# Block-sparse attention and a gated projection on one core: earlier weights, six decoding steps a unit, key blocks copied by GpSimd in every batch, projection steps spread

## The chip, the cores and the metric

The kernel runs on one core of one Trainium2 chip. The metric is the device time of one execution in microseconds (us). The runs shown of the kernel before took 418.15 to 419.96 us, with a median of 419.37 us. Its profile comes from one further execution.

The core has five engines that run their own instruction streams and wait for each other by semaphores: TensorE (PE in the profile; PEld is its weight load), VectorE (DVE), ScalarE (ACT), GpSimd (POOL) and SyncE (SP), which here only issues transfers. Each engine works through its stream in order.

## The reference

For 4 batches, 8 heads, 768 positions and 64 numbers a head, attention is computed under a mask of 24 x 24 blocks of 32 positions. Then the attention's output goes through a causal convolution of five taps that makes a gate, and through two projections.

```python
mask = np.abs(blk_i - blk_j) <= 1
mask |= (blk_i == 0) | (blk_j == 0) | (blk_i == 23) | (blk_j == 23)
for qb in range(24):
    for kb in sampled_blocks[qb]:          # three drawn blocks
        mask[qb*32:(qb+1)*32, kb*32:(kb+1)*32] = True
scores = np.where(mask, q @ k.T / 8, -1e9)
x = softmax(scores) @ v                    # heads side by side: [4, 768, 512]
gate_pre = sum(conv_w[k] * x_padded[:, k:k+768, :] for k in range(5))
out = (sigmoid(gate_pre) * (x @ w_val)) @ w_out
```

So an inner query block sees at most eight key blocks: the two end blocks, itself and its two neighbours, and three drawn ones. The first and last query block see all 24. The drawn numbers are data: the kernel reads them into registers and fetches or copies the blocks that they name. The weights arrive as 64-bit floating numbers and are turned into pairs of 32-bit numbers (high part and rest) on the chip.

## The kernel before

**Units.** The work on attention is cut into 52 units, the passes of the main loop (lines 622 to 678). A batch has 13: four pairs of query blocks, then two units for the end query blocks (unit 4 and 5 of a batch, for which all 24 key blocks are scored), then seven more pairs. With unit `n` the loop issues: loads for pairs some units ahead; the scores of unit `n`; key copies for unit `n + 2` (`COPY_AHEAD`); the values of unit `n - 2` (`LAG_V`), that is probabilities times `v`; and the transposes of unit `n - 1` (`LAG_T`), two blocks for a pair and three for a unit of the end blocks. Behind each transposed block come one call of `fill()` and one of `prepare(steps)`.

**Keys.** For each pair a tile `kg` holds the key blocks that its two query blocks need. Lines 282 and 283 copy four neighbours on GpSimd, line 288 the end blocks on ScalarE. The six drawn blocks come in two ways, by the table `COPIED` (line 39): in batches 0 and 1 GpSimd copies three and ScalarE three out of the batch's whole keys `bt.k`, which are on the chip anyway; in batches 2 and 3 the table is empty, so SyncE fetches each from memory with a transfer of 64 KB (line 272).

**Values.** A pair's own value rows `va` come through SyncE's queue, the drawn ones `vb` by two gathers on GpSimd (line 305). The batch's whole values `vn`, read only by the units of the end blocks, come in three pieces of 520 KB. `V_BEFORE` names the pairs whose key loads they follow: -1 (the end blocks' entry, loaded together with pair 3), 4 and 5.

**Weights.** `load_weights` (line 175) brings eight blocks of 512 KB, four of `w_val` and four of `w_out`, into four staging tiles. The staging tiles `xh`, `xl`, `yh`, `yl` are those that the projections use later. `WEIGHTS_AT` (line 34) gives the unit from which each may be issued, at most one a unit; blocks 4 to 7 wait besides until the block before them in the same tile is decoded. `decode_weights` (line 187) takes eight VectorE steps for the convolution's weights and eight for each block, 72 in all, and begins a block two units after its issue at the earliest. If the next block is not there by the loop's count, the step is lost.

**Projections.** The 768 positions of a batch are cut into tiles of 384 (in the last batch 384, 256 and 128). When a tile's attention is done, `gates` makes its gate (16 VectorE steps of one tap each, and a few that hold only ScalarE work: the first tap and the tanh), and `split` its high part `xh` on ScalarE and its rest `xl` on GpSimd. Neither begins before all weights are decoded. Then `project` takes 11 steps for 384 positions: four value blocks `vp` of 12 matmuls, and for each 128 rows two half output blocks `op` of 6 matmuls; between them VectorE multiplies by the gate (`y`), ScalarE makes `yh` and GpSimd the rest `yl`. One call of `fill()` advances this by one step, one call of `prepare(steps)` does `steps` steps of decoding or, after it, of gates, and one of `split`.

**What sets the order.** Every instruction is chained to the one before it on its engine (`InOrder`, line 59), so the order written is the order run. How much decoding and projecting stands beside which unit is set by four numbers:

```python
STEPS_FIRST, STEPS, STEPS_TAIL, FIRST = 2, 3, 2, 12   # prepare: 2 a call before unit 12, then 3
HELD = (44, 45, 46, 47)                               # units whose later fill() calls are left out
```

By the loop's own count, decoding ends in unit 16, the first gate begins there, and the first value block `vp` is issued in unit 20. The two last loop passes, 52 and 53, have no scores. The work that is left then runs in the loop of lines 679 to 683, with nothing else beside it.

Of the kernel before, what the change touches and what calls it, by code (L numbers as in the profile page):

```python
# [14 lines left out]
SP, POOL, ACT = mybir.EngineType.SP, mybir.EngineType.Pool, mybir.EngineType.Activation  # L15
# [7 lines left out]
CH = 4  # L23
# [4 lines left out]
RING = 4  # L28
VRING = 3
K_AHEAD = (8, 9, 10)  # L30
V_BEFORE = (-1, 4, 5)
GLOB_AFTER = 3
LAG_T, LAG_V = 1, 2
WEIGHTS_AT = (1, 3, 5, 7, 9, 10, 11, 13)
DECODE_LAG = 2
SCALE_AHEAD = 2
COPY_AHEAD = 2

COPIED = [{0: POOL, 1: POOL, 2: POOL, 3: ACT, 4: ACT, 5: ACT}] * 2 + [{}] * 2

STEPS_FIRST, STEPS, STEPS_TAIL, FIRST = 2, 3, 2, 12

HELD = (44, 45, 46, 47)


@with_exitstack
def attention_moe(ctx, tc, qb, kb, v, sampled, w_val, conv_w, w_out, ident_in, slot_in, out):
# [83 lines left out]
    def indices(b):  # L131

        row = const.tile([128, NB], F32, tag=f"row{b % 2}", name="row")
        dve.tensor_scalar_add(row, base, float(b * S - B * S))
        dve.tensor_tensor(out=row, in0=row, in1=valid, op=ALU.mult)
        dve.tensor_scalar_add(idx[:, b, :], row, float(B * S))
# [36 lines left out]
    staged = []  # L173
# [11 lines left out]
    decoded = set()  # L185
# [58 lines left out]
    def block_numbers(pr, eng):  # L244

        mine = [n for n in range(2 * NR) if COPIED[pr.bt.b].get(n, SP) == eng]
        if not mine:
            return
        first = NR * PAIRS[pr.p][0] + mine[0]
        _, regs = nc.values_load_multi_w_load_instructions(  # L250
            sm[0:1, first : first + len(mine)], engines=[eng], min_val=0, max_val=NB - 1,
            skip_runtime_bounds_check_because="block numbers are drawn from [0, 24)",
        )
        for n, reg in zip(mine, regs):
            yield 5 + 4 * (n // NR) + n % NR, reg

    def load_keys(pr):
# [3 lines left out]
        if pr.p == 0 and b == 0:  # L261
            for _ in range(3):
                next(loading[b])
        if pr.p in V_BEFORE:
            next(loading[b])
# [105 lines left out]
    def transposes(un):  # L371
        un.PT = []
        for p in un.P:
            pt = ps_pt.tile([128, 4, 128], F32, tag="pt", name="pt")
            for c in range(4):
                transpose(pt[:, c, :], p[:, 128 * c : 128 * c + 128], ident)
            t = three.tile([128, 4, 128], F32, tag="ptr", name="ptr")
            act.copy(t, pt)
            un.PT += [t[:, c, :] for c in range(4)]
            yield  # L380
# [169 lines left out]
    def store():  # L550
        while stores:
            sp.dma_start(*stores.pop(0))
# [3 lines left out]
    def advance(jobs, after=None):  # L556

        m, g = jobs[0]
        try:
            next(g)  # L560
        except StopIteration:
            jobs.pop(0)
            if after is not None:
                after(m)

    def queue_rows(bt, t):
        m = Rows()
        m.bt, (m.t, m.n), m.ready, m.begun = bt, TILES[bt.b][t], [], False
        to_gate.append((m, gates(m)))
        to_split.append((m, split(m)))  # L570
# [9 lines left out]
    def fill():  # L580
        if to_project and step[0] > max(to_project[0][0].ready):
            advance(to_project)

    def prepare(steps):
        for _ in range(steps):
            if next(decoding, None):
                continue

            if "all" in decoded and to_gate and (to_gate[0][0].begun or len(gating) < 2):
                to_gate[0][0].begun = True  # L590
                gating.add(id(to_gate[0][0]))
                advance(to_gate, prepared)

        if "all" in decoded and to_split and unread <= {id(to_split[0][0])}:
            advance(to_split, prepared)
# [5 lines left out]
    def freed(k):  # L601

        return units[min(k, N - 1)].pr.seq if k >= 0 else -1

    def more(which, upto, load):
        if at[which] < len(pairs) and pairs[at[which]].seq <= upto:
            load(pairs[at[which]])
            at[which] += 1
            return True

    def until(which, n, do):
        while at[which] < min(len(pairs), pairs.index(units[min(n, N - 1)].pr) + 1):
            do(pairs[at[which]])
            at[which] += 1
# [7 lines left out]
    for n in range(N + LAG_V):  # L622
        step[0] = n

        def more_keys():
            return more("keys", freed(n - 1) + RING, load_keys)

        def more_values():
            return more("values", freed(n - LAG_V - 1) + VRING, load_values)

        if n == 0:
            more_keys()
            numbers_first = {eng: list(block_numbers(pairs[0], eng)) for eng in (POOL, ACT)}
            until("scaled", 0, scale)
            indices(0)
            until("copied", 0, copy_keys)
            more_keys()
            until("copied", 1, copy_keys)
            more_values()
        else:  # L640
            while more_keys() or more_values():
                more_values()
        until("scaled", n + (SCALE_AHEAD if n else 1), scale)
        store()
        k = len(staged)
        if k < 2 * CH and n >= WEIGHTS_AT[k] and (k < 4 or k - 4 in decoded):
            next(weights)

        if n < N:
            scores(units[n])  # L650
        if n == 0:
            more_keys()
        until("copied", n + COPY_AHEAD, copy_keys)
        if n == 0:
            while more_keys() or more_values():
                more_values()
        if 0 <= n - LAG_V < N:
            values(units[n - LAG_V])
        steps = STEPS_FIRST if n < FIRST else STEPS
        if 0 <= n - LAG_T < N:  # L660
            for half, _ in enumerate(transposes(units[n - LAG_T])):
                if not (half and n in HELD):
                    fill()
                prepare(steps)
        else:
            fill()
            prepare(steps)
        if 0 <= n - LAG_V < N and units[n - LAG_V].last:
            pr = units[n - LAG_V].pr
            finish(pr)  # L670
            pr.bt.done.add(pr.p)
            for t, (r0, rn) in enumerate(TILES[pr.bt.b]):
                need = {p for p in range(NP - 1) if any(r0 <= i * BLK < r0 + rn for i in PAIRS[p])}
                if r0 == 0 or r0 + rn == S:
                    need.add(-1)
                if t not in pr.bt.queued and need <= pr.bt.done:
                    pr.bt.queued.add(t)
                    queue_rows(pr.bt, t)
# [52 lines left out]
```

## Time and profile before

| what | before |
|---|---|
| runs, median (lowest to highest) | 419.37 us (418.15 to 419.96) |
| profiled execution | 415.0 us, span of its instructions 413.2 us |
| TensorE busy | 342.8 us, 83% of the span |
| weight loads, VectorE, ScalarE, GpSimd busy | 267.8, 274.6, 263.3, 216.3 us |
| transfers | 70.23 MB, mean 170 GB/s |
| key blocks fetched (`kg<-in_k`) | 132 of 64.0 KB |

The profile is of one execution. It counts times from the first instruction. A row of the windows gives a stretch and its length, then for each engine its busy time and number of instructions, then the granted share of TensorE's clock, the busy share of the 16 DMA engines and GB/s. A row of the chain of waits gives start, length and what the chain that ended last was made of there. A group of instructions gives its count, busy time, mean duration in ns, and the idle time of its engine before it with what ended it. All of the kernel's own instructions stand under one line (L65, the helper that chains them), so they are told apart by tile names: `out<-in`. Tiles: `wst` staged weights, `words` the decoder's scratch, `sc` and `s` scores, `mx` their maxima, `pe`, `first`, `rest` probabilities, `pt` and `ptr` their transposes, `av` attention, `th` gates.

### The profile page before, as it was taken

Reading aid. Unit: us, or ns where it says so; the run is one execution under the profiler, and the core shown is the slowest. Engines: PE = TensorE matmul, PEld = TensorE weight load, DVE = VectorE, ACT = ScalarE, POOL = GpSimd, SP = SyncE. Lnnn points to the kernel's source line nnn. Section 1 sums busy time; section 2 is a strip of 40 time slices with the busy share of each in tenths; the row PEclk is TensorE's granted clock in tenths of the full one; section 3 lists DMA queues with packets and bytes.
Section 4 is the critical chain, followed back from the end, with each engine's and each line's share of the span. In section 5 each row is a group of like instructions: output and inputs, shape, how many; then the busy total and the mean of one; then the engine's idle time right before and its main releaser. Section 6 shows DMA issues by size and latency. Waiting matters only on the chain.

```text
span 413.2 us, 16260 instructions
## 1 busy us (share of the span) xinstructions
PE 342.8 (83%) x6640; PEld 267.8 (65%) x6640; DVE 274.6 (66%) x601; ACT 263.3 (64%) x657; POOL 216.3 (52%) x318
## 2 busy tenths in 40 slices
PE   0873877777648999999779999989888899899993
PEld 0442555554335877787559878767756678688992
DVE  4445869899896974965783235985896247957620
ACT  2752778887677796768555656777566565864431
POOL 1864427748557167567634544767266254616240
PEclk9996899998897999999999999999999999999998
DMA  7897367788444245768876376569655563210210
GB/s 239 247 308 226 102 211 227 241 252 246 143 105 155 67 116 171 208 186 261 229 211 196 117 215 185 156 163 334 225 160 153 170 160 115 68 53 26 78 51 25
DMA packets 47522, 70.23 MB, mean 170 GB/s; under 512 B 6232, under 2 KB 29528, under 8 KB 47448
## 3 DMA queue, kind: packets, MB, share of 16 engines
q1 hardware_dynamic: 39976, 45.66, 36.2%
q0 software_dynamic: 7040, 23.43, 19.7%
q8 instruction: 52, 0.85, 0.8%
q14 instruction: 22, 0.18, 0.1%
q10 hardware_dynamic: 432, 0.11, 0.1%
HBM read 62.89 MB, written 6.29 MB: 167 GB/s over the span
## 4 chain that ended last, share of the span: by engine, by line
PE 35%; DVE 28%; DMA 17%; ACT 7%; issue 6%; POOL 3%; SPq 1%; ACTq 0%; POOLq 0%; DVEq 0%
PE vp L65 10%; DVE th L65 10%; PE op L65 9%; DVE mx L65 8%; PE av L65 6%; DMA va<-in_v 5%; PE pt L65 4%; DMA vn<-in_v 4%; PE sc L65 4%; DMA wst<-in_w_val 4%; DVE words L65 4%; ACT pe L65 2%; DVE wst L65 2%; DMA qc<-in_q 2%; POOL yl L65 2%
## 5 line engine op out<-in xcount | busy, mean ns | idle before, releaser
L65 POOL DMA_INDIRECT vb<-in_v,idx x88 | 88.9, 1010 | 82.6 <-PE av L65 49.0
L65 DVE SCALAR_TENSOR_TENSOR th<-xT,cw,th 128x384 f32<-128x384 f32 (+2 forms) x144 | 97.3, 687 | 14.7 <-ACT th L65 11.7
L65 ACT ACTIVATE pe<-sc,mx 128x256 f32<-128x256 f32 x176 | 69.1, 476 | 46.1 <-DVE mx L65 45.9
L65 DVE TENSOR_REDUCE mx<-sc 128x2 f32<-128x512 f32 x88 | 56.5, 683 | 60.5 <-PE sc L65 60.5
L65 PE MATMUL vp<-xh,wv 128*128 128x384 f32 (+2 forms) x288 | 74.7, 331 | 0.0
L65 ACT COPY ptr<-pt 128x512 f32<-128x512 f32 x112 | 64.8, 596 | 14.7 <-PE pt L65 14.4
L65 POOL TENSOR_TENSOR yl<-y,yh 128x384 fp32r<-128x384 f32 (+2 forms) x36 | 35.2, 978 | 71.2 <-ACT yh L65 71.0
L65 PE MATMUL op<-wo,yh 128*128 128x512 f32 x192 | 69.8, 410 | 0.7 <-issue 0.6
L65 PE MATMUL sc<-kg,qc 64*32 64x256 f32 x1408 | 53.4, 410 | 11.8 <-ACT kg L65 10.9
L65 POOL COPY kg<-k 128x256 f32<-128x256 f32 (+1 forms) x154 | 57.9, 414 | 8.7 <-DMA k<-in_k 8.5
L65 PE MATMUL pt<-ident,pe 128*128 128x128 f32 x352 | 54.6, 286 | 7.8 <-ACT rest L65 7.7
L65 PE MATMUL av<-va,ptr 128*32 128x65 f32 x1408 | 47.7, 230 | 10.8 <-DMA va<-in_v 8.1
L65 PEld LDWEIGHTS av<-va,ptr 128*32 128x32 f32 x1408 | 34.0, 114 | 30.8 <-issue 11.3
L65 PEld LDWEIGHTS vp<-xh,wv 128*128 128x128 f32 x288 | 50.8, 188 | 0.2 <-DVE y L65 0.2
L65 PEld LDWEIGHTS pt<-ident,pe 128*128 128x128 f32 x352 | 40.4, 144 | 16.1 <-ACT rest L65 8.8
L65 POOL TENSOR_TENSOR xl<-xT,xh 128x384 fp32r<-128x384 f32 (+2 forms) x36 | 35.2, 979 | 26.1 <-ACT xh L65 24.4
L65 PE MATMUL vp<-xl,wv 128*128 128x384 f32 (+2 forms) x144 | 46.5, 323 | 0.0
L65 PE MATMUL av<-vb,ptr 128*32 128x65 f32 x1408 | 46.4, 226 | 0.0
L65 PE MATMUL op<-wo,yl 128*128 128x512 f32 x96 | 38.3, 399 | 4.3 <-POOL yl L65 4.3
L65 PEld LDWEIGHTS sc<-kg,qc 64*32 64x32 f32 x1408 | 23.3, 111 | 27.2 <-POOL kg L65 12.0
L65 PEld LDWEIGHTS op<-wo,yh 128*128 128x128 f32 x192 | 36.1, 188 | 7.0 <-ACT yh L65 0.6
L65 PEld LDWEIGHTS av<-vb,ptr 128*32 128x32 f32 x1408 | 35.8, 114 | 0.0
(69 smaller groups left out, 449.0 us busy)
## 6 DMA issues: line engine op xcount, KB each, us to landing
kg<-in_k SPq DMA_DIRECT2D x132, 64.0 KB
va<-in_v SPq DMA_DIRECT2D x56, 130.0 KB
vn<-in_v SPq DMA_DIRECT2D x12, 520.0 KB
qc<-in_q SPq DMA_DIRECT2D x48, 128.0 KB
k<-in_k SPq DMA_DIRECT2D x12, 512.0 KB
out<-ot SPq DMA_DIRECT2D x24, 256.0 KB
wst<-in_w_val SPq DMA_DIRECT2D x4, 512.0 KB
wst<-in_w_out SPq DMA_DIRECT2D x4, 512.0 KB
```

Source lines behind the costliest of these rows:

```text
L65: made = getattr(self.eng, name)(*args, **kwargs)
```

## The change

Five things are changed, all in constants and in the main loop.

- `WEIGHTS_AT` lets blocks 0 and 1 be issued in unit 0 and the rest in units 1, 3, 5, 6, 7 and 8. They were 1, 3, 5, 7, 9, 10, 11 and 13. A `while` takes the place of the `if`, so that two can go in one unit.
- `V_BEFORE` moves the three pieces of `vn` behind the key loads of pairs 4, 5 and 6.
- `STEPS_FIRST` and `FIRST` go: `prepare` does three steps a call from the first unit on.
- `COPIED` gives GpSimd the first three drawn blocks of each pair (those of its first query block) in batches 2 and 3 too. SyncE fetches the other three.
- `HELD` becomes every third unit from 17 to 50. In those, only the first of the unit's calls of `fill()` is made.

```diff
-V_BEFORE = (-1, 4, 5)
+V_BEFORE = (4, 5, 6)
...
-WEIGHTS_AT = (1, 3, 5, 7, 9, 10, 11, 13)
+WEIGHTS_AT = (0, 0, 1, 3, 5, 6, 7, 8)
...
-COPIED = [{0: POOL, 1: POOL, 2: POOL, 3: ACT, 4: ACT, 5: ACT}] * 2 + [{}] * 2
-
-STEPS_FIRST, STEPS, STEPS_TAIL, FIRST = 2, 3, 2, 12
-
-HELD = (44, 45, 46, 47)
+COPIED = [{0: POOL, 1: POOL, 2: POOL, 3: ACT, 4: ACT, 5: ACT}] * 2 + [{0: POOL, 1: POOL, 2: POOL}] * 2
+
+STEPS, STEPS_TAIL = 3, 2
+
+HELD = range(17, 51, 3)
...
-        k = len(staged)
-        if k < 2 * CH and n >= WEIGHTS_AT[k] and (k < 4 or k - 4 in decoded):
+        while len(staged) < 2 * CH and n >= WEIGHTS_AT[len(staged)] and (len(staged) < 4 or len(staged) - 4 in decoded):
             next(weights)
...
-        steps = STEPS_FIRST if n < FIRST else STEPS
         if 0 <= n - LAG_T < N:
             for half, _ in enumerate(transposes(units[n - LAG_T])):
                 if not (half and n in HELD):
                     fill()
-                prepare(steps)
+                prepare(STEPS)
         else:
             fill()
-            prepare(steps)
+            prepare(STEPS)
```

With block 0 and 1 in unit 0, SyncE's order there is: queries of pair 0, the batch's keys, queries of pair 1, values of pair 0, weight blocks 0 and 1, then the queries and values of the next pairs.

## The prediction

> **What bounds the kernel now.** A unit is one pass of the main loop, numbered 0 to 51; its start is the first of its score matmuls in the timeline. The loop's order is fixed by hand, so the stages between such starts tell what each part costs. I read the page first (its totals only say that TensorE is busiest), then the windows by stage, then windows by unit, then the chain of waits.
>
> ```profile
> span 413.2 us, 16260 instructions
> PE 342.8 (83%) x6640; PEld 267.8 (65%) x6640; DVE 274.6 (66%) x601; ACT 263.3 (64%) x657; POOL 216.3 (52%) x318
> ```
>
> The stages, with the busy time of TensorE, its weight loads, VectorE, ScalarE and GpSimd, the granted clock and the DMA share. They are units 0 to 5, 6 to 15, 16 to 19, 20 to 50, 51 to 53, and the tail of projections alone:
>
> ```profile
> 10.90:50.10 39.20, 26.42 (x532) 16.43 (x532) 21.73 (x54) 22.71 (x64) 22.78 (x43) 0.87 0.71 217
> 50.10:101.50 51.40, 38.26 (x1127) 27.30 (x1126) 45.25 (x95) 40.70 (x117) 31.34 (x57) 0.97 0.76 238
> 101.50:133.10 31.60, 20.69 (x495) 13.95 (x494) 26.74 (x51) 22.47 (x57) 19.70 (x36) 0.84 0.50 144
> 133.10:354.90 221.80, 207.05 (x4002) 166.47 (x4002) 144.99 (x308) 148.46 (x350) 118.56 (x151) 1.00 0.62 177
> 354.90:370.50 15.60, 14.38 (x279) 11.30 (x279) 11.38 (x24) 10.24 (x24) 7.32 (x7) 1.00 0.21 71
> 370.50:413.20 42.70, 35.97 (x216) 32.27 (x214) 19.51 (x42) 15.78 (x42) 14.47 (x20) 0.96 0.11 44
> ```
>
> The reader is to see two kernels in one. Up to 133 us TensorE has room: 13.1 us of idle time in units 6 to 15 and 10.9 in 16 to 19, while VectorE is 88% busy in the former, on weight decoding. From unit 20, when projections have begun, TensorE is busy 207.05 of 221.80 us. So work that can be done on TensorE before unit 20 shortens the time after it. That needs the weights decoded sooner. Why they are late is in the chain of waits (start, length, what):
>
> ```profile
> 19.45 16.16 DMA wst<-in_w_val
> 35.64 1.03 DVE words L65
> 38.31 0.94 DVE mx L65 x2
> 39.28 1.10 DVE mx L65 x3
> 52.76 0.69 DVE mx L65
> ```
>
> The first weight block is issued at 19.45 and lands at 35.6; VectorE sits in front of it, in program order, with the maxima of unit 4 behind.
>
> The same chain crosses two places in which transfers, not TensorE, end the wait:
>
> ```profile
> 192.45 8.56 DMA vn<-in_v
> 201.63 7.23 DMA qc<-in_q
> 277.09 9.62 DMA vn<-in_v
> 286.73 7.70 DMA va<-in_v
> ```
>
> Both are at the start of a batch (units 28 to 30 and 40 to 42), where six key blocks a pair, the pair's values and the batch's whole values (`vn`) meet on one queue.
>
> Windows by unit give the unit prices. In order: units 8, 9, 10 (four decoding steps each), 13, 14, 15 (six), 24 (six gate steps, two half output blocks), 29, 30 (transfers late), 34 (two half output blocks), 35 (one value block), 36 (two value blocks, six gate steps), 37 (a value block, a half output block, six gate steps), 40 (one half), 41, 42 (two value blocks each, transfers late):
>
> ```profile
> 60.70:64.70 4.00, 3.50 (x111) 2.50 (x110) 3.83 (x10) 3.64 (x12) 1.27 (x2) 1.00 0.34 113
> 64.70:69.60 4.90, 3.51 (x112) 2.51 (x112) 4.73 (x10) 4.25 (x13) 4.43 (x8) 1.00 0.94 272
> 69.60:74.60 5.00, 3.74 (x107) 2.60 (x106) 4.52 (x10) 4.07 (x14) 3.39 (x7) 1.00 0.73 243
> 84.10:89.80 5.70, 3.54 (x107) 2.52 (x106) 5.42 (x15) 4.49 (x14) 1.29 (x2) 1.00 0.95 260
> 89.80:95.70 5.90, 3.62 (x108) 2.53 (x106) 5.69 (x11) 4.65 (x15) 5.43 (x9) 1.00 1.05 339
> 95.70:101.50 5.80, 5.13 (x108) 3.49 (x106) 5.53 (x13) 4.07 (x13) 5.03 (x8) 0.71 0.73 212
> 162.60:168.80 6.20, 6.20 (x122) 4.62 (x121) 6.03 (x12) 3.87 (x11) 4.80 (x6) 1.00 0.60 164
> 196.30:204.80 8.50, 6.19 (x120) 4.70 (x118) 6.64 (x14) 5.06 (x12) 6.55 (x8) 1.00 0.90 237
> 204.80:211.70 6.90, 5.25 (x132) 3.82 (x131) 5.65 (x15) 4.13 (x10) 2.35 (x3) 1.00 0.63 186
> 239.00:245.10 6.10, 6.10 (x119) 4.67 (x118) 2.27 (x6) 3.56 (x9) 2.79 (x5) 1.00 0.68 189
> 245.10:250.60 5.50, 5.50 (x126) 4.66 (x128) 2.19 (x6) 3.40 (x8) 2.66 (x4) 1.00 0.84 229
> 250.60:258.10 7.50, 7.50 (x133) 6.62 (x132) 4.94 (x10) 4.77 (x12) 2.58 (x3) 1.00 0.62 181
> 258.10:264.90 6.80, 6.80 (x125) 5.67 (x124) 6.63 (x14) 5.04 (x13) 4.54 (x6) 1.00 0.58 173
> 278.80:283.60 4.80, 4.80 (x121) 3.69 (x124) 2.31 (x6) 3.55 (x10) 4.17 (x6) 1.00 1.03 381
> 283.60:291.90 8.30, 7.66 (x131) 6.71 (x130) 5.50 (x11) 5.94 (x13) 4.30 (x5) 1.00 0.90 289
> 291.90:301.10 9.20, 7.66 (x131) 6.74 (x130) 7.18 (x14) 5.16 (x12) 3.25 (x4) 1.00 0.62 199
> ```
>
> A plain unit is 3.5 us of TensorE. With one value block it takes 5.5, with two 7.5, so a value block (12 matmuls) is 2.0; one half output block (6 matmuls) makes 4.8 and two make 6.1, so a half is 1.3. The period follows the added work one for one: that is what shows TensorE to be the bound there. Six decoding steps instead of four raise the mean period from 4.63 to 5.80, so a step is 0.58 us while VectorE bounds.
>
> The Trainium skill (Perfetto Trace Analysis, Identifying the Most-Contended Engine) says that matmul busy time is a bad measure of how far TensorE is from its limit, and that weight-load time is a better one; by that, 166.47 of 221.80 us would leave 55 us of room and work moved out would bring nothing. This trace decides against that reading here, by the slope of the periods just given; what is left of it is in the second rival.
>
> **The change part by part.** I count by the loop. A unit calls `prepare` once for each transposed block (twice, three times behind a unit of the end blocks).
>
> *Weights and decoding.* There are 72 decoding steps. Before, 22 are done by the start of unit 6 (2, 4, 2, 4, 4, 6), 44 by the end of unit 11, the last in unit 16. After: 3, 5, 6, 6, 6, 9, that is 35 by unit 6, 70 by the end of unit 11, the last in unit 12. The first tile's gates then run in units 12 to 15, and its first value block is in unit 16 instead of 20.
>
> Units 0 to 5. Blocks 0 and 1 (512 KB each) now go ahead of the queries and values of units 2 and 3. They land before the decoder asks for them in unit 2, and the wait at 35.6 goes. Late next is block 2. Ahead of and with block 0 SP's queue had 4,708 KB (sizes by the shapes in the code); with block 2 it has 5,212, so at this stage's 217 GB/s it lands 2.4 us later, at 38.0. But VectorE has by then done 24 steps instead of 8, and unit 4's maxima too. Behind it stand 11 steps at 0.58, 6.4 us, unit 5's maxima, 2.0 by the two `mx` pieces, and 0.8 of small work: it is free for unit 6's maxima at 47.2, where before they ran at 52.8; as unit 6's scores may be late as well I take 4 of the 5.6. Queued behind the waiting decoder are the maxima, and behind those ScalarE's exponentials and TensorE's transposes. Bounds: -9.5, if VectorE's whole wait for the block goes (its row is in the list of waits below), and +4.8, if the two blocks' 1,024 KB hold everything up at 217 GB/s and nothing is won. **-4.**
>
> Units 6 to 15. Steps: before 2, five times 4, four times 6: 46. After 5, five times 6, then 6, 6, 6, 3 (the last 21 almost all of gates): 56. Ten more at 0.58: **+5.8** (bounds 0, if they fit into VectorE's 6.1 idle us, and +8).
>
> Units 16 to 19 take the first tile's four value blocks and five halves: 4 x 2.0 + 5 x 1.3 = 14.5 us of TensorE beside 20.69, of which the idle 10.9 hides most: 35.2 if nothing idles, 33 to 37 with what overlaps; 35.6, **+4**.
>
> Units 20 to 50 lose these 14.5 and gain the last tile's two halves, 2.6: **-11.9**.
>
> *Projections spread.* Every third unit from 17 to 50 drops one step; none is added or removed. 93 steps in all, and two fewer are left behind unit 50, both halves: units 51 to 53 **-2.6**, the tail of 42.7 unchanged. But in units 23, 29, 38, 41 and 50 one step now meets six (or five) gate steps: TensorE has 4.8 to 5.5, VectorE 6.0 to 6.6 by units 24 and 37. Some 1.1 each, half of it taken up as TensorE may run ahead: **+2.7**.
>
> *Keys.* 66 transfers of 64 KB, 4.2 MB, leave SP's queue. The idle TensorE time of units 29, 30, 41 and 42 is 2.3 + 1.7 + 0.6 + 1.5 = 6.1; I take 1.5 to be left, **-4.6** (bounds 0 and -6.1). In their place 22 pairs get three GpSimd copies each. These rows show their price, and what they do beside VectorE (the groups of instructions, the timelines of the two engines, and the list of waits):
>
> ```profile
> L65 POOL COPY kg<-k 128x128 f32 x66 | 21.0, 350 | 2.4 <-DMA k<-in_k 2.4
> ```
> ```profile
> 257.55 1.93 DVE L65 SCALAR_TENSOR_TENSOR th<-xT,cw,th 128x384 f32<-128x384 f32 x3
> ...
> 269.44 4.32 DVE L65 SCALAR_TENSOR_TENSOR th<-xT,cw,th 128x384 f32<-128x384 f32 x4
> ```
> ```profile
> 249.80 0.74 POOL L65 COPY kg<-k 128x256 f32<-128x256 f32 x2
> ...
> 258.98 1.15 POOL L65 COPY kg<-k 128x256 f32<-128x256 f32 x2
> ```
> ```profile
> DVE words L65 <- DMA wst<-in_w_val: 9.5, 1, 9.5
> ...
> PEld op L65 <- POOL yl L65: 6.7, 6, 1.8
> ```
>
> 3 x 0.35 = 1.05 us a unit, 23.1 in all, against 103 idle us of GpSimd in units 20 to 50. The copies are made two units before their scores; that lead hides them from the scores. Queued behind them on GpSimd are the subtractions (`xl`, `yl`), for which output matmuls already wait in 6 cases, about 1.1 us each: I take **+1.7**; with that cover gone the price is the 23.1.
>
> *End blocks' values.* The three `vn` pieces are issued one to two units later, the last in units 3, 16, 29 and 42, and read first in units 6, 19, 32 and 45. Three units are over 16 us, the longest piece in the chain 9.62, so nothing; if it were late, TensorE would stand in the values. That they leave the first unit is what pays for half of the two weight blocks.
>
> *Sum.* Units 20 to 50: -11.9 - 4.6 + 2.7 + 1.7 = -12.1. In all -4 + 5.8 + 4 - 12.1 - 2.6 = -8.9: a span of 404.3. The profiled execution took 415.0, 1.8 more than its span; so 406.1. The runs shown have a median of 419.37, 4.4 above it; I carry the difference over: 410.5.
>
> **The rivals.** *TensorE's idle time goes altogether* (units 20 to 50 become even, idle falls from the 14.75 to 5, where I left 14.6): 9.6 less, 400.9. For it: units 34 to 37 and 40 show none. Against: GpSimd's subtractions stay.
>
> *VectorE takes back the gain*: no gain in units 0 to 5, and the one-step units cost their full 5.5 with the transfers no better than before: 0 + 5.8 + 4 - 11.9 + 5.5 - 2.6 = +0.8, so 420.2. For it: 88% busy before unit 16, and 6.6 of 6.8 in unit 37.
>
> *GpSimd becomes the bound* in batches 2 and 3: it works in order, and each pair's copies stand before the subtractions, so that up to 23.1 us come onto the path; -8.9 + 23.1 = +14.2, so 433.6. It decides from 11.0 of the 23.1 on, that is in 11 of 22 units. Against it: the 103 idle us. The Trainium skill (SBUF — State Buffer, Who interferes with whom) speaks for it: a VectorE instruction with two inputs in SBUF and a GpSimd one that reads SBUF lock each other out, the later one waiting in full; by that each copy could hold a gate step for its 0.35 us, the same 23.1 us on VectorE. The rows above agree in part: beside subtractions a gate step takes 1.08 us, beside copies and gathers 0.64, and there it is the copy that grows, from 0.37 to 0.58.
>
> That the blocks come too late for six steps a unit (the loop then skips steps) is a weak form of the second rival: only unit 6 loses any by my count.
>
> **How the numbers follow.** Forecast 0.66 (own range 403 to 416), no idle time 0.12, VectorE 0.16, GpSimd 0.06. About 0.5%, 2.1 us, is what a measurement of this kernel can tell from no change. Faster by more: 0.66 + 0.12 + 0.04 of the second rival, 0.82; within 0.11; slower 0.07 (GpSimd, and 0.01). Range: 400 to 417.5; beyond it lie GpSimd's case, the upper half of VectorE's and a little below 400.
>
> **What would show it.** Right: the first decoded block without VectorE idle before it; value blocks from unit 16; units 7 to 11 near 5.8 us; units 16 to 19 near 35.6 with TensorE full; 20 to 50 near 209.7; the tail at 42.7; transfers gone from the chain at the batch starts. Wrong: unit 6 starting after 50, `op` waiting for `yl` by far more than 6.7 us, or score matmuls waiting for GpSimd's keys.

## The result, and the profile after

The changed kernel took 437.89 us (median of 4 runs, 437.44 to 438.95), the kernel before 418.95 us on the same chip (4 runs, 418.15 to 419.96). The ratio is 1.0454, with a 95% interval of 1.0422 to 1.0487: slower, where 410.5 us was forecast. The profiled execution took 438.23 us and its span 436.5 us, beside a forecast span of 404.3.

The page's totals and the stages of the changed kernel (units 0 to 5, 6 to 15, 16 to 19, 20 to 50, 51 to 53, the tail; columns as before):

```profile
span 436.5 us, 16152 instructions
PE 353.8 (81%) x6640; PEld 270.7 (62%) x6640; DVE 288.0 (66%) x601; ACT 262.2 (60%) x657; POOL 230.4 (53%) x384
```
```profile
11.40:50.10 38.70, 26.32 (x532) 15.98 (x532) 26.25 (x65) 23.35 (x65) 23.43 (x40) 0.91 0.83 248
50.10:116.00 65.90, 41.76 (x1127) 29.09 (x1126) 59.26 (x108) 46.31 (x129) 38.06 (x64) 0.92 0.58 176
116.00:154.00 38.00, 34.15 (x573) 26.53 (x572) 23.27 (x47) 25.73 (x64) 21.04 (x36) 0.96 0.33 96
154.00:381.40 227.40, 203.49 (x3939) 157.21 (x3942) 144.62 (x289) 138.94 (x334) 126.69 (x214) 0.99 0.53 156
381.40:395.00 13.60, 13.39 (x275) 10.91 (x275) 9.69 (x22) 9.39 (x22) 4.45 (x4) 1.00 0.30 100
395.00:436.50 41.50, 34.66 (x208) 30.96 (x206) 19.93 (x42) 15.50 (x41) 14.61 (x20) 0.97 0.10 39
```

Units 6 to 15 are 14.5 us longer where 5.8 was forecast, and VectorE is busy 59.26 of 65.90 us. Units 20 to 50, which were to lose 12.1, take 5.6 more, although TensorE's busy time there falls from 207.05 to 203.49 us: its idle time rises from 14.75 to 23.91. The profile of the kernel before was of an execution 4 us below the median of its runs; so the stages' differences add up to some 23 us, where the medians lie 18.9 apart.

The list of waits shows what is new (engine and its instruction, releaser, us in total, times, longest). The wait for the first weight block, 9.5 us before, has no row any more, and `op` waits for `yl` a little more:

```profile
PEld av L65 <- issue: 29.6, 63, 0.8
DVE mx L65 <- remote: 28.8, 7, 7.0
...
PEld op L65 <- POOL yl L65: 9.0, 9, 2.8
```

The first row was 16.2 us in 29 waits before. The second had no row: VectorE's maxima wait for something that the profile cannot name. TensorE's value products look like this in unit 19, in the chain of waits (start, length, what):

```profile
145.32 0.35 PE av L65 x13
145.68 0.32 PE av L65 x5
146.00 0.42 issue
146.42 0.34 PE av L65 x5
146.76 0.42 issue
147.18 1.30 PE av L65 x70
```

TensorE stops in the middle of its value products, waits for nothing that the profile records, and goes on after 0.4 us. The two rows go together. The seven maxima of the second row start 1.3 to 2.6 us after the last score product before them has ended, where most others follow within 0.2 us; the one of unit 19 starts at 147.24, as the last of these pauses ends. Summed over the 52 units, from the first to the last value product of each, these groups take 91.2 us; in the profile of the kernel before they take 71.7.

### The profile page after: what moved, and what is told of

Read it like the earlier page. It is cut to its first block, busy times and chain, and to the rows that moved or that the text cites. A ratio compares the mean times of both kernels' runs of the same rounds, so it can differ in the third digit from the quotient of the medians.

```text
span 436.5 us, 16152 instructions
## 1 busy us (share of the span) xinstructions
PE 353.8 (81%) x6640; PEld 270.7 (62%) x6640; DVE 288.0 (66%) x601; ACT 262.2 (60%) x657; POOL 230.4 (53%) x384
## 2 busy tenths in 40 slices
DMA packets 38017, 65.90 MB, mean 151 GB/s; under 512 B 5176, under 2 KB 20024, under 8 KB 37944
## 4 chain that ended last, share of the span: by engine, by line
PE 46%; DVE 36%; issue 6%; ACT 5%; another core or an unknown queue 2%; POOL 1%; DMA 1%; ACTq 0%; DVEq 0%; POOLq 0%
DVE th L65 12%; PE op L65 11%; PE vp L65 11%; DVE mx L65 10%; PE av L65 8%; PE pt L65 7%; PE sc L65 7%; DVE words L65 5%; DVE wst L65 2%; DVE x L65 2%; DVE rs L65 1%; ACT pe L65 1%; PE xp L65 1%; DVE y L65 1%
## 5 line engine op out<-in xcount | busy, mean ns | idle before, releaser
L65 DVE SCALAR_TENSOR_TENSOR th<-xT,cw,th 128x384 f32<-128x384 f32 (+2 forms) x144 | 106.5, 752 | 14.0 <-ACT th L65 8.5
L65 POOL COPY kg<-k 128x128 f32 (+1 forms) x220 | 73.6, 378 | 9.2 <-DMA k<-in_k 9.1
L65 PE MATMUL sc<-kg,qc 64*32 64x256 f32 x1408 | 55.0, 417 | 16.8 <-POOL kg L65 11.4
L65 POOL TENSOR_TENSOR yl<-y,yh 128x384 fp32r<-128x384 f32 (+2 forms) x36 | 34.6, 962 | 62.2 <-ACT yh L65 62.0
L65 PE MATMUL av<-va,ptr 128*32 128x65 f32 x1408 | 52.5, 233 | 8.0 <-ACT ptr L65 4.0
L65 PE MATMUL av<-vb,ptr 128*32 128x65 f32 x1408 | 51.3, 229 | 4.0 <-issue 3.6
L65 PEld LDWEIGHTS av<-va,ptr 128*32 128x32 f32 x1408 | 35.3, 115 | 30.4 <-issue 14.6
L65 PEld LDWEIGHTS sc<-kg,qc 64*32 64x32 f32 x1408 | 23.2, 112 | 33.3 <-issue 12.7
L65 PE MATMUL op<-wo,yl 128*128 128x512 f32 x96 | 38.7, 403 | 5.6 <-POOL yl L65 5.6
L65 PEld LDWEIGHTS av<-vb,ptr 128*32 128x32 f32 x1408 | 37.8, 116 | 6.3 <-issue 6.2
L65 PEld LDWEIGHTS op<-wo,yh 128*128 128x128 f32 x192 | 36.1, 188 | 7.7 <-ACT yh L65 0.7
```

Of the source, the lines that this page charges most:

```text
L65: made = getattr(self.eng, name)(*args, **kwargs)
```

## The experiments

Eighteen runs in five series, each series on one chip with the kernel before beside it. The kernel before took 410.91, 411.75 and 410.16 us in series 1, 3 and 5, and 417.96 and 419.99 in series 2 and 4, like the 418.95 of the first result: there are two sorts of chip here, and ratios are set against the same chip. In series 1 theory K has GpSimd's new copies push its gathers beside TensorE's value products, theory S has VectorE overfilled before unit 16 by the six steps, and theory H blames the spread steps; later theories are named where they come up. Stages are in us, by the starts of units 6, 16, 20 and 51; `av` is the sum of the value products' groups just told.

| run | series | ratio (95%) | 0-5 | 6-15 | 16-19 | 20-50 | rest | av |
|---|---|---|---|---|---|---|---|---|
| before | first | 1 | 39.2 | 51.4 | 31.6 | 221.8 | 58.4 | 71.7 |
| changed | first | 1.0454 (1.0422 to 1.0487) | 38.7 | 65.9 | 38.0 | 227.3 | 55.1 | 91.2 |
| undo_keys | 1 | 1.0109 (1.0015 to 1.0203) | 36.3 | 64.5 | 36.5 | 208.8 | 55.7 | 71.6 |
| undo_spread | 1 | 1.0347 (1.0257 to 1.0436) | 37.7 | 66.5 | 36.4 | 219.9 | 54.5 | 71.6 |
| undo_steps | 1 | 0.9834 (0.9779 to 0.9889) | 36.9 | 49.2 | 32.2 | 207.9 | 65.2 | 71.1 |
| undo_loads | 1 | 1.0461 (1.0395 to 1.0528) | 38.5 | 57.3 | 31.9 | 218.4 | 70.0 | 69.7 |
| changed_again | 2 | 1.0405 (1.0332 to 1.0479) | 38.8 | 65.9 | 37.9 | 227.1 | 55.1 | 87.8 |
| late_gates | 2 | 1.0223 (1.0152 to 1.0293) | 39.1 | 58.7 | 34.5 | 217.8 | 65.2 | 85.4 |
| plain_gathers | 2 | 0.948 (0.9396 to 0.9563) | 34.7 | 56.2 | 34.0 | 206.0 | 52.5 | 70.1 |
| no_sub | 2 | 1.0071 (1.003 to 1.0111) | 38.8 | 62.5 | 37.7 | 214.3 | 54.4 | 79.4 |
| before_again | 3 | (one run) | 38.5 | 52.0 | 31.2 | 217.9 | 58.3 | 70.1 |
| changed_third | 3 | 1.0291 (1.0263 to 1.0319) | 37.6 | 63.7 | 35.8 | 214.2 | 55.7 | 71.6 |
| undo_keys_again | 3 | 1.0146 (1.0098 to 1.0194) | 36.4 | 66.6 | 35.9 | 210.2 | 55.7 | 72.2 |
| undo_steps_again | 3 | 0.9792 (0.9757 to 0.9827) | 36.1 | 49.8 | 33.8 | 206.3 | 65.2 | 71.2 |
| undo_steps_third | 4 | 0.9948 (0.9922 to 0.9975) | 35.6 | 50.9 | 36.8 | 216.0 | 65.2 | 87.2 |
| sub_dve | 4 | 0.9981 (0.9954 to 1.0009) | 39.1 | 61.1 | 35.2 | 216.5 | 51.7 | 72.5 |
| plain_values | 4 | 459.79 us beside 419.99 | 43.4 | 61.3 | 41.2 | 247.2 | 52.6 | 105.2 |
| plain_values_two | 4 | 1.1144 (1.1066 to 1.1222) | 45.5 | 60.8 | 39.6 | 247.3 | 62.7 | 107.5 |
| two_sub_dve | 5 | 0.973 (0.9671 to 0.979) | 37.2 | 48.5 | 36.1 | 202.8 | 63.2 | 70.6 |
| before_sub_dve | 5 | 0.9943 (0.9898 to 0.9989) | 38.5 | 52.1 | 33.0 | 219.1 | 55.3 | 69.5 |

**Series 1: one part undone at a time.** The edits to the changed kernel:

```diff
# undo_keys
-... + [{0: POOL, 1: POOL, 2: POOL}] * 2
+... + [{}] * 2
# undo_spread
-HELD = range(17, 51, 3)
+HELD = (44, 45, 46, 47)
# undo_steps
-STEPS, STEPS_TAIL = 3, 2
+STEPS_FIRST, STEPS, STEPS_TAIL, FIRST = 2, 3, 2, 12
-prepare(STEPS)
+prepare(STEPS_FIRST if n < FIRST else STEPS)
# undo_loads
-V_BEFORE = (4, 5, 6)
-WEIGHTS_AT = (0, 0, 1, 3, 5, 6, 7, 8)
+V_BEFORE = (-1, 4, 5)
+WEIGHTS_AT = (1, 3, 5, 7, 9, 10, 11, 13)
```

> The changed kernel with the key blocks of batches 2 and 3 fetched by SyncE again, all else changed. Theory K (the copies delay GpSimd, its gathers then run beside TensorE's value products, which took 91.1 us in all instead of 71.6): units 20 to 50 fall from 227.4 to about 213, the value products to about 77 us, total near 424. Theory S (the loss is made by unit 16, where VectorE is full with decoding and gates: 116.0 against 101.5): no change before unit 24, total 436 to 439. Theory H (the spread of projection steps): 436 to 439.

> The changed kernel with the projection steps held back only in units 44 to 47, as before. Theory H (one-step units leave TensorE waiting for VectorE's gates): units 20 to 50 fall by 8 or more, total 430 or less. Theories S and K: unit 16 still starts at 116, units 20 to 50 within 3 us of 227.4, total 435 to 440.

> The changed kernel with four decoding steps a unit in units 0 to 11, weights early. Theory S (VectorE overfilled by the six steps): units 6 to 15 fall from 65.9 to about 55, unit 16 starts near 105, decoding ends in unit 15 instead of 12 and the first value block is in unit 19; total 428 to 431. Theory K: the late part is as before, total 435 to 440, since what the start wins the later projections lose.

> The changed kernel with weights and end blocks' values loaded as before; by the loop's count the decoder then loses 29 steps and ends in unit 16 as before, so that this also undoes most of the early decoding. Theory S: unit 16 starts near 102 as before, total 423 to 426. Theory K: units 20 to 50 still 225 or more (gathers beside value products), total 428 to 434.

Undoing the six steps is what counts: 0.9834, under the kernel before. `undo_loads` is not the loads alone: by the loop's count decoding ends in unit 16 again, and 70.0 us are left behind unit 50. All four runs were also free of the pauses, whichever part was undone, which no theory had said. That made it look as if the pauses needed all parts together; series 3 shows that the chip was the reason. The totals expected above were taken from the first chip and can't be set against these: `undo_keys` and `undo_steps` come out under every total expected of them, and `undo_spread` in theory H's range.

**Series 2: two stages by themselves.** `late_gates` holds gates and split back to unit 16, `plain_gathers` fetches fixed value rows through SyncE's queue, and `no_sub` leaves the low part of the split out.

```diff
# late_gates
-if "all" in decoded and to_gate and ...
+if "all" in decoded and step[0] >= 16 and to_gate and ...
-if "all" in decoded and to_split and ...
+if "all" in decoded and step[0] >= 16 and to_split and ...
# plain_gathers
-pool.indirect_dma_start(out=pr.vb[:, j, :], in_=v, in_offset=idx[...])
+sp.dma_start(pr.vb[:, j, :], v[...])   # 128 fixed rows
# no_sub
-pool.tensor_tensor(out=m.xl[...], in0=xT[...], in1=m.xh[...], op=ALU.subtract)
+pool.memset(m.xl[...].bitcast(F32), 0.0)
```

> The changed kernel as it is, so that the others of this series can be set against it. Theory V (VectorE overfilled before unit 16: units 6 to 15 at 65.9 us where 57.2 was predicted) and theory G (TensorE's value products pause while GpSimd writes the gathers: 91.2 us of value products in all where the kernel before has 71.7) both say that the first run repeats: a ratio of 1.035 to 1.05, units 6 to 15 at 64 to 67 us, units 20 to 50 at 222 to 230 us, value products 86 to 95 us. A rival, chance: the pauses depend on the run, and units 20 to 50 are near 209 us here, with a ratio near 1.00.

> The changed kernel with the first tile's gates and split held back to unit 16, where the kernel before has them; six decoding steps a unit and the early weights stay. By the loop's count the projections of units 20 to 50 and the tail are then those of the run with two steps a call (207.9 and 65.2 us). Theory V: units 13 to 15 fall from 23.2 us to about 13, so units 6 to 15 are 54 to 58 us, units 16 to 19 about 33, units 20 to 50 about 208 if the pauses go as they did in that run: ratio 0.99 to 1.015. Rival (the six decoding steps themselves, with the weights early, are what costs): units 6 to 15 stay at 62 us or more and the ratio is above 1.02. Theory G says of units 20 to 50 only that they are near 225 if the value products still pause.

> The changed kernel with the drawn value rows fetched by plain transfers of the same size on SyncE's queue, from fixed rows, instead of the gathers on GpSimd (leaves out the choice of the rows). Theory G: without gathers on GpSimd the pauses in TensorE's value products go: 70 to 74 us in all instead of 91.2, units 20 to 50 at 206 to 213 us, ratio 0.99 to 1.015. Rival P (pauses have to do with TensorE's own instruction supply or with how the engines happen to stand, not with the gathers): value products stay above 82 us and the ratio above 1.025. Both say that the transfers may come later on SyncE's queue, which would show as waits for va or qc, not as pauses without a wait.

> The changed kernel with GpSimd writing zeros into xl instead of subtracting (leaves out the low part of the split). Theory V with contention (a gate step waits beside GpSimd's two-input subtraction: 929 ns mean in units 6 to 15 where 614 stand alone): the gate step falls to 650 to 720 ns in the mean over the kernel from 818, units 13 to 15 from 23.2 us to 17 to 19, and the kernel by 5 to 10 us. Rival (the number of steps alone overfills VectorE): units 13 to 15 stay above 21 us and the gate step's mean above 780 ns.

The changed kernel repeats within 0.2 us in every stage. Without gates in units 13 to 15, these take 15.7 us instead of 23.2. The theory of VectorE said about 13, and 54 to 58 for units 6 to 15, which took 58.7, so gates account for 7.2 of the 8.7 us by which that stage had exceeded the forecast of 57.2. The ratio stayed above the 1.015 expected; value products still paused, 85.4 us, and units 20 to 50 had been expected without pauses. Without gathers on GpSimd the pauses go (70.1), units 20 to 50 fall by 21.1 us, and units 0 to 15 by 13.8: the gathers, with the waits for free tiles that they bring onto GpSimd (67.9 us behind value products in `changed_again`), cost more than the pauses. The kernel takes 39.5 us less, its value products 17.7. Of the 52 groups of value products in `changed_again`, the 13 that run beside more than 0.3 us of a gather take 19.1 us more than the usual 1.11 or 1.57 us, the other 39 take 7.3 more. Without the subtraction for `xl` the gate step falls from 818 to 717 ns and units 13 to 15 to 19.1 us, about as contention had let expect. The kernel gains more than the 5 to 10 us expected, 16.4; its value products, with 7 groups beside a gather instead of 13, take 8.4 less.

**Series 3: is it the chip?** The kernel before, the changed one and two of series 1 again, on one chip; the edits are those above.

> The kernel before, profiled on the chip of this series, so that its stages stand beside the others without a difference of chips. Both theories: stages 39, 51, 32, 215 to 222 and 58 us; TensorE's value products 70 to 73 us in all.

> The changed kernel on the chip of this series. So far its two profiles, with pauses, and the four profiles with one part undone, without, come from different chips. Theory G (the pauses belong to the changed kernel: they come where all parts together put the gathers beside the value products): value products 86 to 95 us, units 20 to 50 at 222 to 230 us, ratio 1.035 to 1.05. Rival C (the pauses belong to the chip): here they are there in this kernel and in the two below alike, or in none of the three.

> The changed kernel with the key blocks of batches 2 and 3 all fetched again, on the chip of this series. Theory G: value products 70 to 74 us and units 20 to 50 at 206 to 212 us as before, ratio 1.00 to 1.02 beside 1.04 for the changed kernel. Rival C: value products above 82 us if the changed kernel has them so here, and then a ratio within 0.01 of its ratio.

> The changed kernel with two steps a call before unit 12, on the chip of this series. Theory G: value products 70 to 74 us, units 20 to 50 at 206 to 210 us, ratio 0.975 to 0.99. Rival C: value products above 82 us if the changed kernel has them so here, units 20 to 50 at 218 us or more, and a ratio of 1.00 to 1.02.

The theory that the pauses belong to the changed kernel falls: on this chip it has none (71.6 us), and a ratio of 1.0291 instead of 1.0405. Without pauses the parts can be told apart. By the ratios of this chip, four steps instead of six are worth 5.0 points and SyncE's keys 1.5. Of the 15.8 us of span that four steps win here, units 6 to 15 have 13.9; the 7.9 won in units 20 to 50 are less than the 9.5 more behind them. By `undo_spread` and `undo_loads` on the like chip of series 1, the spread steps are worth nothing that the intervals would show, and the early loads, with the early decoding that `undo_loads` loses too, 1.7 points. Units 20 to 50 on this chip, of the kernel before, the changed one and the one with four steps:

```profile
132.20:350.10 217.90, 206.61 (x3997) 166.45 (x3996) 144.53 (x308) 147.95 (x350) 118.23 (x151) 1.00 0.62 181
```
```profile
148.40:362.60 214.20, 197.96 (x3935) 154.82 (x3935) 142.82 (x287) 137.29 (x330) 126.27 (x213) 0.98 0.56 165
```
```profile
131.00:337.30 206.30, 192.85 (x3919) 151.80 (x3918) 131.74 (x291) 139.24 (x335) 133.44 (x217) 1.00 0.59 171
```

From the first to the second TensorE's work falls by 8.65 us, but its idle time rises from 11.29 to 16.24. In the changed kernel 14.1 of that lie in six units: 24, 30, 31, 37, 43 and 44, which in the kernel before have 5.1. Units 24 and 43 in the windows:

```profile
171.80:182.70 10.90, 8.12 (x119) 5.36 (x118) 10.49 (x14) 7.43 (x18) 9.12 (x13) 0.82 0.32 93
305.00:316.00 11.00, 7.47 (x135) 4.66 (x134) 10.61 (x19) 6.83 (x15) 7.43 (x11) 1.00 0.42 118
```

VectorE is busy for 10.49 of 10.90 us and TensorE is not. What VectorE does there is in the chain, and what GpSimd does meanwhile in its timeline:

```profile
178.34 4.13 DVE th L65
182.47 0.02 issue
182.49 0.63 DVE th L65
```
```profile
174.30 1.13 POOL L65 DMA_INDIRECT vb<-in_v,idx  x1 [0.16 <-issue]
175.73 1.03 POOL L65 DMA_INDIRECT vb<-in_v,idx  x1 [0.30 <-issue]
176.77 1.44 POOL L65 COPY kg<-k 128x256 f32<-128x256 f32 x5
178.18 0.98 POOL L65 TENSOR_TENSOR yl<-y,yh 128x384 fp32r<-128x384 f32 x1
179.13 1.00 POOL L65 TENSOR_TENSOR xl<-xT,xh 128x384 fp32r<-128x384 f32 x1
180.09 0.99 POOL L65 TENSOR_TENSOR yl<-y,yh 128x384 fp32r<-128x384 f32 x1
181.05 0.99 POOL L65 TENSOR_TENSOR xl<-xT,xh 128x384 fp32r<-128x384 f32 x1
```

One gate step takes 4.13 us: it lasts until the fourth of GpSimd's subtractions has ended, and the next one takes 0.63. GpSimd was late behind two gathers and five copies, so its subtractions came in a run.

**Series 4: waits or number, and no gathers.** `sub_dve` moves the subtractions for `xl` and `yl` to VectorE. `plain_values` fetches the right drawn rows by eight transfers of 32 rows a pair with addresses from registers (it also makes the table of row numbers, and rows of zeros behind the values), `plain_values_two` the same with four steps.

```diff
# sub_dve
-pool.tensor_tensor(out=m.xl[...], ...)
+dve.tensor_tensor(out=m.xl[...], ...)
-pool.tensor_tensor(out=yl[...], ...)
+dve.tensor_tensor(out=yl[...], ...)
# plain_values
-pool.indirect_dma_start(out=pr.vb[:, j, :], in_=v, in_offset=idx[...])
+for s, reg in enumerate(regs):     # four row numbers, loaded into SyncE's registers
+    sp.dma_start(pr.vb[32 * s : 32 * s + 32, j, :], v[bass.ds(reg, 32), :])
```

> The changed kernel with two steps a call before unit 12, once more, as the mark for the two versions below and, if the chip of this series is one on which value products pause, to see whether they pause here too. Theory L (a gate step waits for a whole run of GpSimd's subtractions, which six steps a unit bring about in units 13 to 15, 24, 30 and 42): gate step 690 to 710 ns in the mean, ratio 0.975 to 0.99. Rival (on a chip with pauses it pauses as the changed kernel does): value products above 82 us and ratio 1.00 to 1.02.

> The changed kernel with all subtractions for xl and yl on VectorE instead of GpSimd; nothing is left out. Theory L: with no two-input instruction on GpSimd the gate step falls from 827 ns to 615 to 640 ns in the mean; units 13 to 15 take 20 us or less instead of 23.2, unit 24 at most 9 us instead of 10.9, and in spite of 56 more instructions of about 0.6 us on VectorE the kernel is 3 to 10 us under the changed one, ratio 1.00 to 1.02 on a chip without pauses. Rival N (the number of steps alone overfills VectorE): units 13 to 15 at 23 us or more and a ratio of 1.03 or more.

> The changed kernel with the right drawn value rows by plain transfers: eight blocks of 32 rows a pair on SyncE's queue with register addresses, no gathers on GpSimd, zero rows at the end of the values for what is masked. Theory G in its present form (gathers cost their time on GpSimd, hold its copies and subtractions back, and on some chips pause TensorE): ratio 0.95 to 0.98 on any chip, value products 69 to 73 us. Rival (352 small transfers with register loads are too many for SyncE, values come late): waits of av for vb transfers above 15 us in all, ratio 0.99 or more.

> The kernel above (value rows by plain transfers) with two steps a call before unit 12. Theory L: without gathers GpSimd is less late, so six steps cost less than the 0.05 that they cost beside gathers; this one is 0.01 to 0.03 under the one above, 0.94 to 0.96. Rival (with GpSimd free the six steps bring their projections forward as the prediction wanted): this one is 0.005 or more above the one above.

This chip has pauses, and the version with four steps has them too: 87.2 us of value products, units 20 to 50 at 216.0. It still beats the kernel before, by 0.5%. With the subtractions on VectorE, where one takes 0.55 us in the median instead of 1.0, the gate step is down from 827 to 650 ns (615 to 640 were expected), as these groups show (before_again, changed_third and sub_dve, in this order; busy us, mean ns):

```profile
L65 DVE SCALAR_TENSOR_TENSOR th<-xT,cw,th 128x384 f32<-128x384 f32 x112 | 81.3, 738 | 13.6 <-ACT th L65 11.2
```
```profile
L65 DVE SCALAR_TENSOR_TENSOR th<-xT,cw,th 128x384 f32<-128x384 f32 x112 | 91.1, 827 | 12.5 <-ACT th L65 10.2
```
```profile
L65 DVE SCALAR_TENSOR_TENSOR th<-xT,cw,th 128x384 f32<-128x384 f32 x112 | 71.5, 650 | 11.8 <-ACT th L65 7.4 <-issue 1.2 <-ACT yh L65 1.1
```

But units 13 to 15 fall only to 21.3 us, not to 20, and unit 24 takes 11.7. So both theories hold a part. In units 13 to 15 VectorE is busy with the 16 gate steps for 10.29 us instead of 14.63 in `changed_third`, 4.3 less, but four subtractions of 0.6 us each now stand on it. Where the subtractions for `xl` were left out and nothing took their place (`no_sub`), these units took 19.1 us: so the waits are about 4 of the 5.8 us more than in the kernel before, and the rest is not told apart. In unit 24 the wait is not what counts: without it VectorE does 11 gate steps there, of 0.63 us each, and the unit is no shorter. The low value products (72.5) go with only 4 groups beside a gather. With both, the kernel comes to 0.9981 on this chip, where without the edit it had 1.0405 and 1.0454 on others of the slower sort. `plain_values` lost: 459.79 us, and the chain of its page has 17% of SyncE's sequencer, where `plain_gathers` has 0%:

```profile
PE 38%; DMA 18%; SPq 17%; issue 10%; DVE 7%; ACT 6%; POOL 3%; ACTq 0%; POOLq 0%; DVEq 0%
```
```profile
vb<-in_v SPq DMA_DIRECT2D x352, 65.0 KB, 2.3
```

The rival was right: 352 transfers with register loads, where `plain_gathers` had 88, are too many in SyncE's order. The value products wait for `vb` for 19.6 us, part of the 105.2 that they take, and the queries stand behind the transfers (VectorE waits for them for 47.2 us). What the number of transfers costs and what the register loads cost is not told apart. `plain_values_two` took 469.01 us, 2% more than with six steps, as its rival had said; so that four steps are better is shown only for kernels with the gathers. What `plain_gathers` shows is the price of the gathers, not a kernel.

**Series 5: the subtractions alone.**

> The changed kernel with two steps a call before unit 12 and all subtractions for xl and yl on VectorE; nothing is left out. Theory L and N together (too many VectorE steps before unit 16, and gate steps that wait for GpSimd's subtractions) give both gains: units 6 to 15 at 48 to 50 us, gate step below 660 ns, ratio 0.96 to 0.985. Rival (VectorE pays for the subtractions what it saves in waits, so only the four steps count): ratio 0.98 to 0.995, as with four steps alone.

> The kernel before with all subtractions for xl and yl on VectorE and nothing else. Theory L: the gate step falls from 738 to 620 to 660 ns, output matmuls wait less for yl, ratio 0.975 to 0.995. Rival (the before kernel's gates wait where VectorE is not the bound, so it is worth nothing there): ratio 0.995 to 1.01.

The edit is worth 0.6% on the kernel before, by an interval that just leaves out nothing at all (gate step 643 ns). With four steps it gives 0.973, the best version here, 400.03 us beside 410.16. Four steps alone gave 0.9834 and 0.9792 on the two like chips; the intervals overlap, so what the edit adds there is not settled.

## Why the prediction was wrong

*The bound.* TensorE does bound units 20 to 50 while nothing stands in its way, and the version with four steps shows 192.85 us of work in 206.30 there. The inference that fell is that work moved ahead of unit 20 shortens the time by its length.

*Units 0 to 5, forecast -4, measured -0.5.* The wait for the first weight block went, as said. VectorE's time took its place: it is busy 26.25 of 38.70 us, where it was 21.73 of 39.20. And what the upper bound of +4.8 was worked out from came true in part: unit 4's scores start at 34.6 us instead of 26.6. On the chip of series 3 (33.6 instead of 26.1) the chain of `changed_third` shows the queries behind the two blocks, where the kernel before had the wait for the weight block:

```profile
4.68 9.59 DMA va<-in_v
14.29 12.30 DMA qc<-in_q
```

In the first chip's chain no transfer stands there, but for 5.20 us a maximum that waits for what the profile cannot name.

*Units 6 to 15, forecast +5.8, measured +14.5. The step that failed is "Ten more at 0.58".* It priced gate steps as decoding steps ("the last 21 almost all of gates"). Units 6 to 12, where by the loop's count 13 steps are added, nine of them of decoding, took 8.7 us more on the first chip and 5.8 on that of series 3, beside 7.5 at 0.58. Units 13 to 15 have, by the loop's count, 15 gate steps where 18 decoding steps were. At 0.58 that is 1.7 less; it was 5.8 more, on both chips. The first row below has the 16 gate steps that the trace shows in units 6 to 15 (busy us, mean ns), all of them in 13 to 15, whose windows follow:

```profile
L65 DVE SCALAR_TENSOR_TENSOR th<-xT,cw,th 128x384 f32<-128x384 f32 x16 | 14.6, 929 | 2.0 <-ACT th L65 1.7
```
```profile
92.80:100.50 7.70, 3.77 (x107) 2.54 (x106) 5.84 (x14) 6.46 (x18) 2.36 (x3) 1.00 0.46 129
100.50:108.70 8.20, 3.81 (x111) 2.57 (x110) 8.02 (x12) 6.24 (x18) 7.73 (x13) 1.00 0.75 212
108.70:116.00 7.30, 5.08 (x107) 3.62 (x106) 7.09 (x12) 4.91 (x14) 5.62 (x8) 0.77 0.79 236
```

Gates bring first taps, tanh and high parts on ScalarE (busy 6.46 of 7.70 us in unit 13) and subtractions on GpSimd, beside which VectorE waits (8.02 of 8.20 busy in unit 14). `late_gates` takes 7.5 us away there, `no_sub` 4.1. So a gate step took 0.93 us where 0.58 was put, and the prediction had such a price in its own rows: 1.08 us beside subtractions.

*Units 16 to 19, forecast +4, measured +6.4*, and 4.6 on the chip without pauses: right but for these.

*Units 20 to 50, forecast -12.1, measured +5.6.* On the chip without pauses it is -3.7. So of the miss of 17.7, 8.4 is the forecast's own, and 9.3 is what the first result adds in this stage. The transfers left the chain, as forecast; the shares of the chain by engine, before and after:

```profile
PE 35%; DVE 28%; DMA 17%; ACT 7%; issue 6%; POOL 3%; SPq 1%; ACTq 0%; POOLq 0%; DVEq 0%
```
```profile
PE 46%; DVE 36%; issue 6%; ACT 5%; another core or an unknown queue 2%; POOL 1%; DMA 1%; ACTq 0%; DVEq 0%; POOLq 0%
```

But TensorE's work fell by 8.65 instead of 11.9, and its idle time rose by 4.9 where the forecast had 0.2 less (-4.6 + 2.7 + 1.7). The term mis-sized is "some 1.1 each, half of it taken up" for gate steps in and behind the one-step units: units 24, 30, 31, 37, 43 and 44 idle for 14.1 us together. Series 1 doesn't lay this on the spread alone, since undoing it won nothing: there the six units idle for 7.4 us, but others more, 22.58 in all. With four steps, which put the gates elsewhere, the six idle for 8.0 and the stage for 13.45.

*Units 51 on, forecast -2.6, measured -3.3.* Right.

*The rivals.* GpSimd's case gave 433.6, near the result, and by another way: `op` waited 9.0 instead of 6.7 us for `yl`, not 23.1. On chips without pauses "VectorE takes back the gain" is the mechanism, and it was under-priced at 420.2: 1.0291 of 419.37 is 431.6. The Trainium skill (SBUF — State Buffer, Who interferes with whom) has a VectorE instruction with two inputs in SBUF and a GpSimd instruction that reads SBUF lock each other out. The forecast weighed this for GpSimd's copies; it tells most at the subtractions. In `changed_third` 18 gate steps that run mostly beside an `xl` subtraction take 1.25 us in the median and up to 4.20, the 11 beside copies 0.63, the 35 alone 0.62. For subtractions the trace agrees that the later one waits in full; for copies it agrees in part. Six of the 11 steps take 0.63 us and five 0.73 to 2.41, and 12 copies of two blocks beside gate steps take 0.62 us in the median, where 35 with no VectorE work beside them take 0.40.

*The pauses* had no place in the forecast. They are shown to need gathers on GpSimd (they go with `plain_gathers` on a chip that has them), and they came only on chips of one of two sorts. The maxima's wait without a name stands in the first profile of the changed kernel and in every profile with gathers of series 2 and 4, and in no other. Why only some chips stays open. The profile of the kernel before shows neither, although 18 of its groups run beside a gather; but its chip isn't known, and its 415.0 us lie between all other runs of this kernel on the one sort (407.81 to 414.83) and on the other (416.03 to 422.86). No profile is known to show the kernel before on the slower sort, so whether it pauses there is open too.

## What to carry to other kernels

A step's price belongs to its kind and to what the other engines run at that moment: price gates from a stage with gates (here 0.93 us a step, not 0.58), and count what they bring along on ScalarE and GpSimd. Before moving work ahead, ask whether the engine that must prepare it has room there; here VectorE was 88% busy and the early steps cost more than the moved work was worth. Undo the parts one at a time, on one chip: here the six steps cost 5%, the key copies 1.5%, the spread nothing that shows, and undoing the two changes of the loads together made the kernel slower.

## What the runs showed of the hardware

- The same kernel took 410 to 412 us in three series, each on a chip of its own, and 418 to 420 in two others and in the first result, whose chip isn't known. On the slower sort three different versions paused in value products beside gathers (85.4 to 91.2 us instead of 70 to 72), mostly by 0.4 to 0.5 us at a time and with no recorded wait, and VectorE's maxima started up to 2.6 us after the scores had ended.
- A VectorE gate step of 0.62 us stood for 4.13 us until four GpSimd subtractions of 1.0 us had ended. The same subtraction takes 0.55 us in the median on VectorE.
- With 352 transfers of 65 KB and addresses from registers SyncE's sequencer was 17% of the chain and the kernel took 459.79 us; with 88 of 260 KB and fixed addresses it was 0%, and 397.56 us on another chip.
